# V's loads moved from SP's queue to ACT's in a cached attention decode kernel

## The chip, the cores and the metric

The kernel runs on one core of a Trainium2 chip. The metric is the device time of one execution in microseconds (us), median of several runs. Below, PE is TensorE (PEld its weight loads), DVE is VectorE, ACT is ScalarE, POOL is GpSimd and SP is SyncE. A transfer is issued by an engine, on that engine's own queue, and is carried out by the core's 16 DMA engines.

## The reference

For a batch of 2 with one new token each, the output is a gated mix of two branches:

```
g   = sigmoid(sum(x * gate_w))
a   = attention(x): q = x @ wq, 32 heads of 128
      p = softmax(q . k_cache / sqrt(128)) over 16384 cached positions
      a = (p @ v_cache) @ wo
b   = mlp(x): layernorm, w1, gelu, shifted w2, residual, layernorm, w3, gelu, w4, residual
out = g * a + (1 - g) * b
```

All inputs are bf16. `k_cache` and `v_cache` have the shape (2, 32, 16384, 128), 268 MB each: 573 MB are read with the weights, and each cached element is used once.

## The kernel before

**Units.** The work on the caches is cut into 32 units: 16 pairs of heads (`hp`) by 2 batch elements (`b`). A unit has one K transfer (`load_k`) and one V transfer (`load_v`) of 8.39 MB, each 128 rows of 64 KB, one to a partition. In the text a unit with b=0 is an even unit and one with b=1 an odd unit; K(hp,b) and V(hp,b) are their loads.

**Memory.** One SBUF tile `mem` is split into five cells of half a load. K of an even unit takes cells 0 and 1, K of an odd unit cells 1 and 2, so they share cell 1. V always takes cells 3 and 4. So K of the next unit can be loaded when the half of the present K that is in the way has been read, and V of the next unit when PV of the present one has read the cell.

**A unit's steps.** `score_first` and `score_second` go over K in halves: DVE turns a chunk (L408, eight to a unit), PE multiplies it with the spread-out query (L414) and sums into a PSUM tile S. `softmax_a` (L435 to L439) turns S, takes the maximum and writes the matrix `Dm` on ACT; `softmax_b` (L445 to L462) spreads the maximum over the partitions, makes the exps on ACT (L452) into `pt`, and takes the reciprocal of their sum on DVE (L462). `pv` (L468) is 64 matmuls of `pt` with V into `oacc`. `pv_end` evicts `oacc` on ACT (`osb`, L481) and sums it by matmuls (L486).

**Order.** The order of each engine is the program's (`in_order` ties each instruction to the one before it on its engine). The scores of one unit come ahead of PV of the unit before: after K of unit u has landed, the order is `score_first(u)`, the issue of K(u+1), `score_second(u)`, `softmax_a(u)`, `pv(u-1)`, the issue of V(u), `pv_end(u-1)`, `softmax_b(u)`. The loop `For_i` runs 15 times over `odd_rest` (from the second half of an odd unit) and `even_unit`; in its last round `last_unit` is added, and V(15,1) goes to cells 0 and 1.

**Queues.** All of K, V and the large weights are issued by SP, on its queue, in program order. An issue waits on SP until its place in `mem` is free (L112 for K, L117 for V). ACT issues only the two small inputs `xin` (L85) and `gwT` (L87) at the start. Before the loop, SP issues w1, w2, wq, K(0,0), w3, K(0,1) and V(0,0); after V(15,1) come wo and W4 in five pieces (`load_apart`, L526), which wait for PV of the units whose cells they take.

Of the kernel before, what the change touches and what calls it, by code (L numbers as in the profile page):

```python
# [23 lines left out]
def kernel(  # L24
# [15 lines left out]
    nc = tc.nc  # L40
    P = nc.NUM_PARTITIONS
    B, Sq, D = A_x.shape
    _, H, Sk, Dh = A_k_cache.shape
# [10 lines left out]
    NJ = 2 * Sk // P  # L54
# [25 lines left out]
    def region(cell, elements, offset=0):  # L80
        at = cell * CELL + offset
        return mem[:, at : at + elements]
# [24 lines left out]
    def cache_rows(cache, hp, b):  # L107
        two = cache[b, bass.ds(2 * hp, 2)]
        return two.rearrange("h s d -> (h s) d").rearrange("(p j) d -> p (j d)", p=P)
# [4 lines left out]
        )  # L114

    def load_v(hp, b, cell=V_CELL):
        nc.sync.dma_start(out=region(cell, NJ * Dh), in_=cache_rows(A_v_cache, hp, b))  # L117


    ident_f = const.tile([P, P], FP32)  # L120
# [3 lines left out]
        out=ident_s[:], in0=ident_f[:], scalar1=-scale, scalar2=None, op0=ALU.mult  # L124
# [10 lines left out]
        out=mask4[:], in_=mask4[:], compare_op=ALU.is_ge, fill=0.0,  # L135
# [3 lines left out]
        out=mask4[:], in_=mask4[:], compare_op=ALU.is_ge, fill=0.0,  # L139
# [11 lines left out]
        out=lmat[:].rearrange("p (g h k) -> p g h k", h=2, k=4),  # L151
        in_=hm2[:].unsqueeze(1).unsqueeze(3).to_broadcast([P, P // 8, 2, 4]),
# [5 lines left out]
        out=lane[:],  # L158
        in_=ident_f[:].rearrange("p (c k) -> p k c", k=QP),
# [5 lines left out]
    for g in range(Q4):  # L165
        nc.vector.tensor_scalar(
            out=spread[:, g],
# [161 lines left out]
    for k in range(2):  # L329
        wide = mlp.tile([P, 16, QP], FP32, tag="wide", name="wide")  # L330
        nc.scalar.activation(
            out=wide[:].rearrange("p (c e) i -> p c e i", e=2),
            in_=oacc[k][:].rearrange("p (c i e) -> p c e i", i=QP, e=2),
# [15 lines left out]
    for e in range(2):  # L349
        half = slice(e * HALF, (e + 1) * HALF)  # L350
        nc.vector.tensor_copy(
            out=qdu[half].rearrange("p u v -> p (u v)"),
            in_=qdps[half, e].rearrange("p k g n -> p (k g n)"),
# [212 lines left out]
    softmax_a(0)  # L566
    mlp_third(w3)
    load_v(0, 0)
    softmax_b(0)
    score_first(0, 1)  # L570
# [3 lines left out]
    def odd_rest(hp):  # L574
        loads.append(load_k(hp + 1, 0))
        score_second(1)
        softmax_a(1)
        pv(0)
        load_v(hp, 1)
        pv_end(hp, 0)  # L580
        softmax_b(1)

    def even_unit(hp):
        score_first(hp, 0)
        loads.append(load_k(hp, 1))
        score_second(0)
        softmax_a(0)
        pv(1)
        load_v(hp, 0)
        pv_end(hp - 1, 1)  # L590
        softmax_b(0)
        score_first(hp, 1)
# [89 lines left out]
```

## Time and profile before

| | |
|---|---|
| time, median of 3 runs | 1332.62 us (1332.56 to 1332.70) |
| the profiled execution's own time | 1332.68 us |
| its span, first to last instruction | 1330.5 us |
| busy: PE, DVE, ACT, POOL | 57%, 49%, 10%, 1% |
| read from HBM | 572.53 MB, 430 GB/s over the span |
| issue to landing, median: K, V | 28.0 us, 31.7 us |
| granted TensorE clock, mean | 0.794 |

The profile gives one execution. Its timeline lists instructions with their start, how long they took and, in brackets, how long the engine stood idle before and what ended that. `SPq` is SP issuing or waiting. A DMA's time to landing runs from its issue until its data is there, and includes the time behind other transfers. The trace also holds a record of every DMA packet with start, duration, size and queue; q1 is SP's queue and q10 is ACT's.

### The profile page before, as it was taken

The page shows a single profiled execution, that of the slowest core. Times are in us where ns is not written, and L with a number is a line of the kernel's source. Part 1 is how long each engine was busy: PE and PEld are TensorE (multiplying, and loading weights), DVE is VectorE, ACT ScalarE, POOL GpSimd, SP SyncE. Part 2 cuts the span into 40 slices and gives each one's busy share as a digit, 9 for nine tenths or more (in the row PEclk, how much of TensorE's full clock was granted, in tenths as well). Part 3 has the DMA queues.
Part 4 walks back from the last instruction along what each step waited for, and adds up shares of the span by engine and source line. Part 5 has one row for each costly group of instructions (what it writes and reads, how often), then busy time and mean ns, then how long its engine had stood idle before and what let it go on. Part 6 is the DMA issues. An engine that isn't in the chain of part 4 may idle for free.

```text
span 1330.5 us, 12949 instructions
## 1 busy us (share of the span) xinstructions
PE 763.4 (57%) x4992; PEld 330.0 (25%) x4992; DVE 654.0 (49%) x515; ACT 130.4 (10%) x204; POOL 13.0 (1%) x47
## 2 busy tenths in 40 slices
PE   1455666565556656555665655566565556656553
PEld 1222222222222222222222222222222222222222
DVE  2454455554445555444555544455554445555420
ACT  0011100011110001111000111110011111001110
POOL 1000000000000000000000000000000000000000
PEclk9777887687888868788886777888777788877776
DMA  9999999999999999999999999999999999999997
GB/s 410 432 434 426 436 437 433 428 435 437 435 426 435 437 435 426 435 437 435 426 435 437 435 426 435 437 435 428 433 437 437 426 433 437 437 426 433 437 437 333
DMA packets 11086, 572.69 MB, mean 430 GB/s; under 512 B 1602, under 2 KB 1602, under 8 KB 1988
## 3 DMA queue, kind: packets, MB, share of 16 engines
q1 hardware_dynamic: 10660, 572.53, 99.5%
q8 instruction: 8, 0.13, 0.0%
q10 hardware_dynamic: 416, 0.01, 0.0%
q14 instruction: 2, 0.02, 0.0%
HBM read 572.53 MB, written 0.00 MB: 430 GB/s over the span
## 4 chain that ended last, share of the span: by engine, by line
DMA 46%; PE 9%; DVE 8%; issue 5%; PEld 1%; DVEq 0%; ACT 0%; SPq 0%; PEldq 0%; ACTq 0%
DMA mem<-in_A_k_cache_dram 42%; PE S L414 8%; DVE KT L408 8%; DMA mem<-in_B_w_dram 2%; DMA mem<-in_A_v_cache_dram 2%; PE oacc L468 1%; PEld L414 0%; PEld misc L486 0%; ACT osb L481 0%; PEld misc L461 0%; SPq L112 0%; DVEq L408 0%; DVEq L641 0%; PEld misc L445 0%; DVEq L677 0%
## 5 line engine op out<-in xcount | busy, mean ns | idle before, releaser
L414 PE MATMUL S<-KT,qw 128*128 128x512 bf16 x2048 | 557.7, 424 | 354.9 <-DVE KT L408 348.4
L408 DVE STREAM_TRANSPOSE KT<-mem 128x2048 f32<-128x2048 f32 x256 | 574.2, 2287 | 270.6 <-DMA mem<-in_A_k_cache_dram 180.2
L414 PEld LDWEIGHTS <-qw 128*128 128x128 bf16 x2048 | 221.7, 108 | 686.0 <-issue 515.8
L468 PE MATMUL oacc<-mem,pt 128*8 128x512 bf16 x2048 | 118.9, 386 | 7.3 <-DMA mem<-in_A_v_cache_dram 7.3
L439 ACT ACTIVATE Dm<-ident_s,m 128x128 f32<-128x128 f32 x32 | 12.9, 402 | 979.1 <-PE oacc L468 915.0
L452 ACT ACTIVATE pt<-St,nb 64x256 bf16<-64x256 f32 x64 | 89.7, 1401 | 58.8 <-DVE nb L450 57.9
L490 DVE TENSOR_SCALAR o_all<-misc,g_rep 128x2 f32 (+1 forms) x32 | 7.0, 219 | 163.5 <-PE misc L486 163.5
L461 PE MATMUL misc<-rs,lmat 128*128 128x1 f32 x64 | 18.8, 362 | 106.8 <-ACT pt L452 61.2
L468 PEld LDWEIGHTS <-pt 128*8 128x8 bf16 x2048 | 47.5, 87 | 75.8 <-issue 24.3
L486 PE MATMUL misc<-lane,osb 128*128 128x2 f32 x256 | 33.3, 252 | 45.2 <-ACT osb L481 45.2
L462 DVE RECIPROCAL rinv<-misc 128x1 f32<-128x1 f32 x32 | 5.4, 168 | 107.4 <-PE misc L461 104.2
L435 DVE STREAM_TRANSPOSE St<-S 128x512 f32<-128x512 f32 x32 | 22.9, 716 | 66.2 <-PE L468 64.2
L486 PEld LDWEIGHTS misc<-lane,osb 128*128 128x128 f32 x256 | 31.0, 191 | 60.9 <-ACT osb L481 31.6
L461 PEld LDWEIGHTS misc<-rs,lmat 128*128 128x128 f32 x64 | 16.0, 311 | 113.1 <-ACT pt L452 64.8
L481 ACT ACTIVATE osb<-oacc,rinv 128x512 f32<-128x512 f32 x32 | 22.0, 687 | 88.6 <-PE oacc L468 88.6
L452 ACT ACTIVATION_READ_ACCUMULATOR pt<-St,nb 64x1 f32 x64 | 30.5, 477 | 0.0
L357 POOL TENSOR_TENSOR qw<-qdu,mask 128x16 bf16<-128x16 bf16 x32 | 8.5, 267 | 1162.4 <-PE L468 1089.8
L450 DVE TENSOR_REDUCE nb<-misc 64x1 f32<-64x64 f32 x64 | 14.2, 222 | 4.8 <-PE misc L445 0.7
L445 PE MATMUL misc<-Dm,ones_f 128*128 128x128 f32 x64 | 15.4, 323 | 0.0
L370 PE MATMUL arow<-mem,o_turned 128*2 128x256 bf16 x128 | 5.9, 361 | 14.7 <-DMA mem<-in_A_wo_dram 8.9
L437 DVE TENSOR_REDUCE m<-St 128x1 f32<-128x256 f32 x32 | 13.4, 420 | 1.1
L551 DVE CAST out_row<-arow 2x256 bf16<-2x256 f32 x2 | 0.8, 414 | 26.1 <-PE arow L370 26.1
(85 smaller groups left out, 73.6 us busy)
## 6 DMA issues: line engine op xcount, KB each, us to landing
mem<-in_B_w_dram SPq DMA_DIRECT2D x1, 7168.0 KB, 32.6
mem<-in_B_w_dram SPq DMA_DIRECT2D x2, 2048.0 KB, 12.2
mem<-in_B_w_dram SPq DMA_DIRECT2D x1, 3840.0 KB, 41.3
mem<-in_B_w_dram SPq DMA_DIRECT2D x1, 1792.0 KB, 30.8
mem<-in_B_w_dram SPq DMA_DIRECT2D x1, 768.0 KB, 32.2
mem<-in_A_k_cache_dram SPq DMA_DIRECT2D x32, 28.0
mem<-in_A_v_cache_dram SPq DMA_DIRECT2D x32, 31.7
mem<-in_B_w_dram SPq DMA_DIRECT2D x1, 512.0 KB, 33.0
```

The costliest lines, as they stand in the source:

```text
L408: nc.vector.transpose(out=kt[:], in_=Kc.rearrange("p j d -> p (j d)").bitcast(FP32))
L414: nc.tensor.matmul(S, lhsT=qw[b][:, v, NG - 1 - m : NG - 1 - m + P], rhs=ktb[:, half * GT : (half + 1) * GT, w, :, e], start=(first and n ...
L435: nc.vector.transpose(out=st[:].rearrange("p j r -> p (j r)"), in_=S[:])
L437: nc.vector.tensor_reduce(out=m[:], in_=st[:, :, 0:NG], axis=AX.XY, op=ALU.max)
L439: nc.scalar.activation(out=Dm[:], in_=ident_s[:], func=ACTF.Copy, scale=m[:, 0:1])
L445: nc.tensor.matmul(R_ps[:], lhsT=ones_f[:], rhs=Dm[:], start=True, stop=True)
L450: nc.vector.tensor_reduce(out=nb[rows], in_=R_ps[rows, rows], axis=AX.X, op=ALU.min)
L452: nc.scalar.activation(out=pts[b][rows, :, e, :].rearrange("p (m a) k -> p a k m", a=GT // 4), in_=st[rows, :, 0:NG].rearrange("p (a k) m ...
L461: nc.tensor.matmul(tot_ps[:], lhsT=lmat[:], rhs=rs[:], start=True, stop=True)
L468: nc.tensor.matmul(oacc[b][QP * q : QP * q + 8, :], lhsT=pts[b][:, g].rearrange("p h k -> p (h k)"), rhs=V[:, 4 * g : 4 * g + 4, :].rearra ...
L481: nc.scalar.activation(out=osb[:], in_=oacc[b][:], func=ACTF.Copy, scale=rinvs[b][:, 0:1])
L486: nc.tensor.matmul(ot[:], lhsT=osb[:, k * Dh : (k + 1) * Dh], rhs=lane[:, k : k + 5 : 4], start=(k == 0), stop=(k == 3),)
```

## The change

`load_v` issues its transfer from ACT in the place of SP. Source, destination, size and the place in the program's order stay; the waits on V's cell stand on ACT now, in ACT's order. All 32 V transfers are meant, V(15,1) in `last_unit` too. K's and the weights' transfers stay with SP.

```
     def load_v(hp, b, cell=V_CELL):
-        nc.sync.dma_start(out=region(cell, NJ * Dh), in_=cache_rows(A_v_cache, hp, b))
+        nc.scalar.dma_start(out=region(cell, NJ * Dh), in_=cache_rows(A_v_cache, hp, b))
```

## The prediction

> **What bounds the kernel now.** I read the page first: DMA share by slice, the queues, the chain.
>
> ```profile
> DMA  9999999999999999999999999999999999999997
> ...
> q1 hardware_dynamic: 10660, 572.53, 99.5%
> ...
> DMA mem<-in_A_k_cache_dram 42%; PE S L414 8%; DVE KT L408 8%; DMA mem<-in_B_w_dram 2%; DMA mem<-in_A_v_cache_dram 2%; PE oacc L468 1%; PEld L414 0%; PEld misc L486 0%; ACT osb L481 0%; PEld misc L461 0%; SPq L112 0%; DVEq L408 0%; DVEq L641 0%; PEld misc L445 0%; DVEq L677 0%
> ```
>
> SP's queue (q1) fills the 16 DMA engines for 99.5% of the span, and every slice but the last reads nine tenths. No compute engine passes 57%. The kernel is DMA-bound; its time changes only if the DMA engines stand empty for longer or shorter, or move bytes at another rate. What is empty now is 0.5% of 1330.5, 6.7 us, and it lies at the two ends: nothing moves before 1.8 us or after the last weight piece (below).
>
> Next, what the queue waited for (SP's waits), and one odd unit (b=1) and the even one after it in the timeline:
>
> ```profile
> SPq L112 <- DVE KT L408: 489.0, 31, 23.4
> SPq L117 <- PE oacc L468: 345.7, 30, 17.8
> ```
>
> ```profile
> 477.08 4.51 DVE L408 STREAM_TRANSPOSE KT<-mem 128x2048 f32<-128x2048 f32 x2 [6.87 <-DMA mem<-in_A_k_cache_dram]
> ...
> 487.76 0.34 SPq L112 DMA_DIRECT2D mem<-in_A_k_cache_dram  x1
> ...
> 501.83 3.63 PE L468 MATMUL oacc<-mem,pt 128*8 128x512 bf16 x64
> ...
> 506.12 0.33 SPq L117 DMA_DIRECT2D mem<-in_A_v_cache_dram  x1
> ...
> 512.15 0.17 DVE L462 RECIPROCAL rinv<-misc 128x1 f32<-128x1 f32 x1 [3.35 <-PE misc L461]
> 515.78 4.51 DVE L408 STREAM_TRANSPOSE KT<-mem 128x2048 f32<-128x2048 f32 x2 [3.46 <-DMA mem<-in_A_k_cache_dram]
> ...
> 525.88 0.33 SPq L112 DMA_DIRECT2D mem<-in_A_k_cache_dram  x1
> ```
>
> Read from K's landing (477.08): the next K is issued 10.7 us later, when half of this K is transposed (10.1 to 11.5 over the units); PV runs 24.8 later, V is issued 29.0 later, DVE is free 35.2 later. Landings are 38.70 us apart, two loads of 19.35: the queue always holds the next load while one moves. Each load is 128 rows of 64 KB, so 8 packets per DMA engine at 2.42 us.
>
> Last, what two queues do to each other, in the DMA queues' view and in stretches of time (last two columns: DMA share, GB/s; a packet counts whole where it starts):
>
> ```profile
> xin<-in_A_x_dram ACTq DMA_DIRECT2D x1, 4.0 KB, 12.9
> gwT<-in_gate_w_dram ACTq DMA_DIRECT2D x1, 2.0 KB, 31.8
> ```
>
> ```profile
> 0.80:1.80 1.00, 0.00 (x0) 0.00 (x0) 0.38 (x4) 0.00 (x0) 0.79 (x5) 1.00 0.00 0
> 1.80:2.20 0.40, 0.00 (x0) 0.00 (x0) 0.28 (x4) 0.00 (x0) 0.40 (x2) 1.00 3.02 573
> ...
> 13.00:32.40 19.40, 6.10 (x72) 3.85 (x72) 4.66 (x25) 0.98 (x3) 1.41 (x2) 1.00 1.00 433
> ```
>
> 2 KB on ACT's queue took 31.8 us: its 9 small packets per engine each waited for one large packet of SP's. So the engines take turns, one packet from each queue. While that went on (13.0 to 32.4) SP's rate was the usual 433 GB/s: turning costs nothing that shows. SP's first issue is at 0.80 and the first packet follows in the 1.80 stretch: 1.0 us from issue to motion.
>
> **The change, part by part.**
>
> *Issue cost.* 32 transfers leave SP and join ACT. Each is 0.33 us of DMA_DIRECT2D with a register move (0.03) and a register operation (0.07): 0.43 us on ACT, 13.8 us in all, on an engine busy for 10%. ACT's wait before V (PV's end) is the one its next instruction, the eviction osb at L481, has anyway (506.11 against V's 506.12); behind it stand osb, the exps and so the reciprocal. That path ends 35.2 after K's landing, 3.5 before the next K, so 0.43 would hide there. In the new order (below) it holds up K's transposes in even units, and V's seventh packet covers it; uncovered, 16 × 0.43 = 7. On SP, K's issue loses the V wait ahead of it, worth nothing: K's last wait was for DVE (row one).
>
> *Order of the bytes.* This carries the sum. Before, K and V moved one after the other; now whichever overlap share packet by packet, so a K takes up to twice as long, and either queue can run dry alone. The engines stand empty only when both are dry: V's queue is dry from V's last byte until PV is over, K's from K's last byte until half of K is transposed. Worked through in packets:
>
> At the start: w3 ends at 70.1, K(0,1) then moves, V(0,0) (issued at 77.9, moving at 78.8) joins when K has 4 packets left. Eight alternating packets, 19.4 us, bring K in at 99.6 instead of 89.96, and V has 4 left, 9.7 us, until 108.8. K(1,0) can't move before 99.6 + 10.9 + 0.9 = 111.4. Empty: 2.6.
>
> In the loop, with 0 the last byte of an odd unit's K (0.47 before DVE starts, by the packet records), and V having 5 packets left, to 12.1:
> - Next K moves at 0.47 + 10.8 + 0.9 = 12.2 (0.9 lies between 1.04 for the first weight and 0.74 for the output in the packet records), alone: V is issued at 29.5 and moves at 30.4, in K's last packet. K lands at 31.6.
> - V moves alone with 8 packets. The even unit can't start: DVE is free at 35.2 + 0.47 = 35.7, 36.1 with ACT's 0.43. Its next K moves at 36.1 + 10.6 + 0.9 = 47.6, waits for V's seventh packet (48.5), alternates with the eighth; V lands at 53.4.
> - PV waits for the scores and V is issued 25.4 after the unit's start (24.9 to 26.1 in even units), at 61.5, and moves at 62.4, within K's fifth packet (to 63.1). Three K and three V packets alternate: K lands at 77.6, V has 5 left. The pattern repeats; 77.6 against 77.4 before.
>
> So an odd unit's V is drained at 12.1 and K comes at 12.2 in the middle, 11.5 to 13.0 at the ends of the rows: empty 0 to 0.9, mean near 0.2. After a standstill the first packets are slow: 0.95 to 1.76 us at the start of the run against 0.61 for the same size later, so 0.3 to 1.1 more; I take 0.35 on average, since often K comes without a full stop. 14 odd units after the first: 14 × 0.55 = 7.7. The start costs 2.6 + 0.5 = 3.1. Sum +10.8.
>
> The price of issue to motion decides. The Trainium skill ("DMA: Bandwidth & Descriptors", section "Latency and other measured facts") puts a first byte from SP or ACT at about 0.6 us; the rows here show 0.74 and 1.04. By 0.6, K would come at 11.9, before V has drained, and only the start's 2.8 would remain, 1335.5; I go by the rows.
>
> *Tail.* V(15,1) now shares with wo instead of going before it. PV of it ends before wo and the first W4 piece are through (28 us), so the later pieces still come in time: zero; if that cover fails, PV's 6.5 us plus 1 of issue.
>
> **Rivals.**
> 1. *No change* (within 0.2%, 2.7 us, about what a measurement of this kernel can tell from no change). K reaches the engines before 12.1, or K's turn comes slightly more often than V's, and the loop never runs dry: 0 to 2.6 for the start, about 1334.5. For it: K came at 11.5 in some units. Against: the middle is over 12.1, and one standstill delays K and feeds the next. The Trainium skill's rule in the same page ("Issuing engines are not separate DMA queues") also gives no change: all issuers' transfers run on the same 16 engines and interleave, only issue time is saved. The xin row bears out the interleaving; the rule says nothing of when a queue runs dry.
> 2. *Much slower.* One V packet fewer is left at the odd landing (4, drained at 9.7): K is 2.5 late plus 0.5 of refill, in 14 units, 42, with the start 45: 1378. It decides if V's next load moves a packet earlier, before 60.6 instead of 62.4, or if engines share finer than by packets: in even shares without whole packets the same steps give 1.5 to 2.0 per pair, 21 to 28 and the start, near 1360.
> 3. *Faster.* Two queues fill gaps between packets of one. Against: 8 × 2.419 is 19.35, there are no gaps between loads; the 6.7 us empty now lie where one transfer or none is under way. If the first 1.8 and half the 4.7 after the last byte came back, -4: 1328.5, but V's queue touches neither end.
> 4. *The transfers stay in one order whatever the queue*: the time stays, 1332.7. The gwT row speaks against it; its chance is in "no change".
>
> **How the numbers follow.** Forecast 0.55, rival 2 0.20, no change 0.17, faster 0.08. The profiled execution took 1332.68 (span 1330.5, 2.2 around it), the median is 1332.62, so no correction: 1332.7 + 10.8 = 1343.5. Its own bounds: issue to motion of 0.74 with no refill gives +3.5; 1.3 with 0.5 gives +17. The range, 1333.5 to 1365, takes in the upper part of "no change" and the finer sharing. Faster 0.08, same 0.17, slower 0.75.
>
> **What would show it.** V on ACT's queue (q10) with 268 MB; landings of K in turn about 32 and 46 us apart instead of 38.7; K's time to landing near 20 and 31, V's 24 and 28; slices around 430 GB/s; a first K landing in the loop near 99.6. Wrong if landings still come every 38.7 (one order), if DMA slices hold 433 all along (no change), or if they drop under 425 (rival 2).

## The result and the profile after

The time goes from 1332.66 us to 1357.21 us (medians of 4 runs each; the change ranges from 1355.97 to 1357.46): ratio 1.0182, interval 1.0170 to 1.0195. It is slower, by 24.6 us where 10.8 were forecast. The profiled execution took 1357.46, span 1355.3, 24.8 more than the one before.

The page of the changed kernel: DMA share and rate by slice, the two queues, the chain.

```profile
DMA  9999989999999999999999999999999999999998
GB/s 403 431 437 403 434 371 433 433 429 433 406 433 402 433 433 429 435 404 433 426 435 408 433 433 433 433 402 433 433 433 433 402 433 433 433 404 435 435 427 342
...
q1 hardware_dynamic: 6052, 304.09, 52.7%
q10 hardware_dynamic: 5024, 268.44, 45.9%
...
DMA mem<-in_A_k_cache_dram 49%; DVE KT L408 9%; PE S L414 7%; DMA mem<-in_B_w_dram 2%; DMA mem<-in_A_v_cache_dram 2%; PE oacc L468 0%; PEld L414 0%; DVEq L408 0%; DVEq L641 0%; PEld misc L486 0%; SPq L112 0%; PEld misc L461 0%; DVEq L677 0%; DVE out_row L551 0%; PE arow L370 0%
```

V's 268 MB are on ACT's queue (q10). Most slices still move 433 GB/s, but nine between the first and the last drop to 371 to 408. The DMA queues' view shows that K now takes longer to land (28.0 before) and V less (31.7 before):

```profile
mem<-in_A_k_cache_dram SPq DMA_DIRECT2D x32, 32.3
mem<-in_A_v_cache_dram ACTq DMA_DIRECT2D x32, 29.2
```

The timeline around an odd unit, the even one after it and the next odd one:

```profile
652.75 4.50 DVE L408 STREAM_TRANSPOSE KT<-mem 128x2048 f32<-128x2048 f32 x2 [11.54 <-DMA mem<-in_A_k_cache_dram]
...
663.55 0.34 SPq L112 DMA_DIRECT2D mem<-in_A_k_cache_dram  x1
...
676.46 3.63 PE L468 MATMUL oacc<-mem,pt 128*8 128x512 bf16 x64
...
680.76 0.34 ACTq L117 DMA_DIRECT2D mem<-in_A_v_cache_dram  x1
681.28 0.69 ACT L481 ACTIVATE osb<-oacc,rinv 128x512 f32<-128x512 f32 x1 [2.92 <-PE oacc L468]
...
687.28 0.17 DVE L462 RECIPROCAL rinv<-misc 128x1 f32<-128x1 f32 x1 [3.35 <-PE misc L461]
688.00 4.50 DVE L408 STREAM_TRANSPOSE KT<-mem 128x2048 f32<-128x2048 f32 x2 [0.55 <-DMA mem<-in_A_k_cache_dram]
...
731.54 4.50 DVE L408 STREAM_TRANSPOSE KT<-mem 128x2048 f32<-128x2048 f32 x2 [11.57 <-DMA mem<-in_A_k_cache_dram]
```

DVE starts on K at 652.75, 688.00 and 731.54: 35.3 and 43.5 apart where both were 38.7. The pair takes 78.8 instead of 77.4. osb starts 0.52 after V's issue on ACT. What happens just after 663.55 is seen in stretches of the same execution (last two columns: DMA share, GB/s; a packet counts whole in the stretch it starts in):

```profile
655.00:663.90 8.90, 8.28 (x27) 3.07 (x27) 6.87 (x4) 0.00 (x0) 0.00 (x0) 0.74 0.82 353
663.90:664.50 0.60, 0.60 (x5) 0.24 (x4) 0.00 (x0) 0.00 (x0) 0.00 (x0) 1.00 0.01 0
664.50:665.10 0.60, 0.60 (x4) 0.17 (x2) 0.00 (x0) 0.00 (x0) 0.00 (x0) 1.00 3.90 1311
```

By the packet records, the last V packets end one engine after the other from 663.8 to 664.4, and no packet of a load starts in the second row's 0.6 us. From 664.5 to 665.6 the 16 engines take up the K that SP issued at 663.55. This comes back once in every pair, and the first K packets are slow then: 12 to 16 of the 16 take over 0.3 us more, and the mean over the pairs is 3.06 us instead of 2.42 (0.64 more). In the same execution, the first packets of a K that joins a running V (703.7, even unit) are not slow: 2.42 us.

The records show one thing more. A load is complete when each engine has also served a 4-byte packet behind its data, and that packet takes its own turn in the queue. With one queue K landed 0.1 us after its last data; here, wherever V is moving, the small packet waits behind one 64 KB packet of V (2.41 us), and K lands 2.7 to 2.8 us after its last data. The sum over the middle of the run, in stretches from 110 to 1280 us, before and then after:

```profile
110.00:1280.00 1170.00, 695.88 (x4282) 298.49 (x4281) 599.41 (x426) 118.91 (x184) 7.76 (x29) 0.80 1.00 433
```

```profile
110.00:1280.00 1170.00, 672.10 (x4168) 290.74 (x4168) 584.59 (x416) 116.90 (x180) 7.70 (x29) 0.80 0.99 425
```

8 of 433 GB/s over 1170 us are 21.6 us. The share falls by only 0.01, because an engine with a slow first packet counts as busy.

### The profile page after: what moved, and what is told of

It reads as the page before. It is cut to its first block, busy times and chain, and to the rows that moved or that the text cites. A ratio compares the mean times of both kernels' runs of the same rounds, so it can differ in the third digit from the quotient of the medians.

```text
span 1355.3 us, 13000 instructions
## 1 busy us (share of the span) xinstructions
PE 755.5 (56%) x4992; PEld 329.2 (24%) x4992; DVE 651.7 (48%) x515; ACT 130.4 (10%) x204; POOL 12.9 (1%) x47
## 4 chain that ended last, share of the span: by engine, by line
DMA 53%; DVE 9%; PE 8%; issue 4%; PEld 0%; DVEq 0%; SPq 0%; PEldq 0%; ACTq 0%
DMA mem<-in_A_k_cache_dram 49%; DVE KT L408 9%; PE S L414 7%; DMA mem<-in_B_w_dram 2%; DMA mem<-in_A_v_cache_dram 2%; PE oacc L468 0%; PEld L414 0%; DVEq L408 0%; DVEq L641 0%; PEld misc L486 0%; SPq L112 0%; PEld misc L461 0%; DVEq L677 0%; DVE out_row L551 0%; PE arow L370 0%
## 5 line engine op out<-in xcount | busy, mean ns | idle before, releaser
L414 PE MATMUL S<-KT,qw 128*128 128x512 bf16 x2048 | 548.0, 417 | 375.7 <-DVE KT L408 370.4
L439 ACT ACTIVATE Dm<-ident_s,m 128x128 f32<-128x128 f32 x32 | 12.9, 402 | 990.4 <-PE oacc L468 908.6
L206 DVE STREAM_TRANSPOSE turn<-wide 128x256 f32<-128x256 f32 (+2 forms) x5 | 3.4, 685 | 18.1 <-ACT wide L331 10.7
(85 smaller groups left out, 78.4 us busy)
## 6 DMA issues: line engine op xcount, KB each, us to landing
mem<-in_B_w_dram SPq DMA_DIRECT2D x2, 2048.0 KB, 12.2
mem<-in_A_k_cache_dram SPq DMA_DIRECT2D x32, 32.3
```

The source lines that it names most:

```text
L414: nc.tensor.matmul(S, lhsT=qw[b][:, v, NG - 1 - m : NG - 1 - m + P], rhs=ktb[:, half * GT : (half + 1) * GT, w, :, e], start=(first and n ...
L439: nc.scalar.activation(out=Dm[:], in_=ident_s[:], func=ACTF.Copy, scale=m[:, 0:1])
```

## The experiments

**Theory A**: the queues take packets in turn; in an odd unit both run dry before the next K moves, the engines stand and restart slowly. **Rivals**: B, V's issue on ACT and what stands behind it makes the loss; C, two transfers under way at once move fewer bytes per us. D to H name rivals of single runs. The rate below is that of 110 to 1280 us.

### K and V exchanged: e1_swap and e12_swap_loop

```
     def load_k(hp, b):
-        return nc.sync.dma_start(
+        return nc.scalar.dma_start(            # V: nc.sync, as before
```

> K's transfers on ACT's queue, V's back on SP's: still two queues, but no V issue on ACT. Theory A (the two queues take packets in turn, and both run dry in an odd unit before the next K moves): the loss stays, 1350 to 1361 us, with standstills and K landings about 35 and 43.5 us apart. Rival B (ACT's 0.4 us of issue ahead of the eviction, 32 times, and what stands behind it, makes the loss): about 1333 to 1340, as K's issue stands where ACT has nothing to do. Rival C (two transfers under way at once move fewer bytes per us): as A in time, but with a rate under 433 GB/s in the stretches without a standstill.

Measured: 1377.9 us (1372.5 to 1381.6), ratio 1.0335. Outside A's range too: K(0,1) now waits in ACT's order, and the engines are empty from 32.1 to 40.3 and from 77.1 to 90.3. After that most pairs are 78.4 to 78.9 us long. So it was run again with K(0,0) and K(0,1) on SP (`load_k` now takes the issuing engine as an argument):

```
-    load_k(0, 0)
+    load_k(0, 0, nc.sync)                      # and load_k(0, 1, nc.sync)
```

> As e1_swap (K on ACT's queue, V on SP's), but the two K loads ahead of the loop stay on SP, since in e1_swap they waited in ACT's order and left the engines empty for 7.9 and 13 us before 91 us. A: the loop's pairs stay 78.5 us long and the whole is 1352 to 1360 us. B (the loss is ACT's issue of V ahead of the eviction): 1333 to 1340.

Measured: 1357.5 us (1356.3 to 1361.8), ratio 1.0183 (1.0168 to 1.0199), the changed kernel's own. V isn't issued by ACT here at all, so B falls: the loss belongs to two queues, not to V's issue on ACT. The row is of the slowest of the four executions, 1361.8 us.

```profile
110.00:1280.00 1170.00, 665.66 (x4144) 287.02 (x4144) 577.97 (x413) 116.90 (x180) 7.72 (x29) 0.80 0.99 423
```

### The next K later: e4_late_k, and on one queue e5_late_k_one_queue

```
-        score_chunks(b, halves[1 - b], True, False)
+        score_chunks(b, [0, 1, 2, 4] if b else halves[1], True, False)
...
     def odd_rest(hp):
+        score_chunks(1, [3], False, False)
         loads.append(load_k(hp + 1, 0))
-        score_second(1)
+        score_chunks(1, [5, 6, 7], False, True)     # the same in last_unit
```

> The changed kernel with one other chunk of K scored ahead of the last chunk of the shared cell in odd units, so that the next K is issued one chunk and the loop's turn later, 4.6 us. A: the standstill of 0.4 grows to about 5 us per pair where whole packets don't hide some: 30 to 60 us on top, 1385 to 1415 us. B and C: nothing about ACT or about shared movement changes, 1357 to 1360.

> The control to e4_late_k: the same later issue of K (4.6 us in odd units) with all on SP's queue. A: V is under way when K is issued, so the 4.6 us are hidden: 1332.5 to 1333.5 us. If a later K costs by itself (E), 15 x 4.6: about 1400 us.

Measured: e4 1391.0 us (1389.9 to 1394.0), ratio 1.0443, 33.8 more than the changed kernel; e5 1338.4 (1334.3 to 1339.6), ratio 1.0043. The slices of e4 show the larger standstills, in rates down to 336 GB/s and shares of seven and eight tenths:

```profile
DMA  9998979999999999989999999989999999999997
GB/s 416 428 427 373 440 336 442 404 423 423 393 423 404 442 393 423 440 376 451 395 423 393 423 423 393 438 378 451 395 423 425 404 440 387 429 393 423 453 421 336
```

In the loop they are mostly 2 to 3 us by the packet records, against 0.3 to 0.8. The wait for the next K is therefore the price in two queues, as A has it. The control missed slightly: one queue hides most of the 4.6 us, but 1.7 to 7 us remain. A likely reason, argued and not shown: K then moves about 17 us after the last byte, and the engine that is 2.1 us ahead of the last one has drained its V at 17.3.

### V in smaller packets: e2_half_v, e3_quarter_v, e11_half_v_one_queue

```
     def load_v(hp, b, cell=V_CELL):
-        nc.scalar.dma_start(out=region(cell, NJ * Dh), in_=cache_rows(A_v_cache, hp, b))
+        rows = cache_rows(A_v_cache, hp, b)
+        n = NJ * Dh // 2                            # // 4 in e3; nc.sync in e11
+        for k in range(2):
+            nc.scalar.dma_start(out=region(cell, n, k * n), in_=rows[:, k * n : (k + 1) * n])
```

> The changed kernel with each V load cut into two halves along the row, 32 KB packets in the place of 64 KB: in turns of one packet K moves 64 KB for V's 32, so V lasts longer beside K. A: V still has packets when the next K comes in every unit, the standstills go, 1332 to 1336 us. B: 32 more issues on ACT, 1357 or up to 14 more. C: as many bytes or more move beside each other, 1357 or more.

> The changed kernel with each V load in four quarters, 16 KB packets: V gets a fifth of the engines while K moves, so V ends late, PV and the next V wait for it, and K runs alone and dry. A: slower than the changed kernel, 1365 to 1430 us, estimated by steps in packets. B: 96 more issues on ACT at 0.4 us, 1357 to 1395, with no late V. C: about 1357 (the bytes that move beside each other change little).

> The kernel before, all on SP's queue, with V in two halves along the row (32 KB packets): what the smaller packets cost by themselves. In e2_half_v a 32 KB packet took 1.213 us against half of 2.4194, 1.2097: over 8192 packets on 16 engines 1.7 us, up to the 3.1 that its records sum to. So 1334.4 to 1336 us if the rest of e2_half_v's 13 us comes from its two queues (A); 1343 to 1346 if halves cost that much on any queue (D).

Measured: e2 1346.1 us (1343.4 to 1348.3), ratio 1.0105; e3 1349.5 (1346.4 to 1356.0), ratio 1.0142; e11 1334.6 (1334.5 to 1334.8), ratio 1.0015 (1.0006 to 1.0024). So halves cost 2.0 by themselves, and two queues with halves lose 11.5 more, less than half of the changed kernel's loss. That is right in direction, short in size: long standstills are gone (none over 0.3 us in e2's loop, as a mean over the 16 engines), but many engines still drain V just as K comes, and 142 K packets are over 0.3 us slow (223 in the changed kernel). Halves do two things, and these runs don't separate them: V lasts longer beside K, and K's completion waits behind 32 KB of V (1.21 us) in the place of 64 KB (2.41). In e3 my estimate was wrong: V doesn't end late, since it has the engines to itself while the next K waits. In its profiled execution (13.7 us over before) 9.7 are the 16 KB packets' own: 0.614 us each against 0.605, a quarter of 2.4194. B and C don't fit either: more issues on ACT, or as much sharing, made it faster.

### Half a K ahead of time: e6_split_k, e14_split_k_one_queue, e16_split_even_k, e17_split_odd_k

```
     def load_k(hp, b):
-        return nc.sync.dma_start(
-            out=region(K_CELL[b], NJ * Dh), in_=cache_rows(A_k_cache, hp, b)
-        )
+        rows = cache_rows(A_k_cache, hp, b)
+        parts = []
+        for k in (b, 1 - b):                        # the half for the cell that only this K uses, first
+            parts.append(nc.sync.dma_start(
+                out=region(K_CELL[b], CELL, k * CELL), in_=rows[:, k * CELL : (k + 1) * CELL]))
+        return parts
```

e6 has V in halves on ACT too; e14 has V whole on SP. e16 splits only K of b=0 (e17: of b=1), with V whole on ACT:

```
+        cells = ((b,), (1 - b,)) if b == 0 else ((0, 1),)      # one DMA for each group of cells; e17: b == 1
```

> The changed kernel with K loaded in halves by cell: the half for the cell that no other K uses is issued as soon as that cell is read, before the present K has landed; the other half as before. V in halves too, so that packets stay of one size. SP's queue then always holds half a K when V has drained. A: no standstills, no slow restarts in the loop: 1333 plus 2 x 3 for the 32 KB packets plus up to 3 at start and tail, 1336 to 1343 us. C (two transfers under way at once are slower): 1357 or more.

> The control to e6_split_k: K in halves by cell, all on SP's queue, V whole. Only the smaller packets cost, as V's halves did (2.0): 1334 to 1335.5 us. Then e6_split_k's 5.2 us are 4.0 of packets and about 1 that two queues cost where neither runs dry.

Measured: e6 1337.8 us (1336.8 to 1338.1), ratio 1.0038 (1.0025 to 1.0051); e14 1334.7 (1334.6 to 1334.9), ratio 1.0015 (1.0006 to 1.0024). K and V are still on two queues and under way together, yet the rate is back:

```profile
110.00:1280.00 1170.00, 716.14 (x4210) 303.37 (x4209) 594.80 (x422) 116.87 (x180) 7.73 (x29) 0.80 1.00 432
```

By the packet records no stretch of e6's loop is empty. C falls. Of its 5.2 us, 2.0 and 1.9 are the halves (e11, e14); 1.3 are left for two queues that don't run dry.

> The changed kernel with only the K loads of even units in halves by cell (those that are issued in odd units), the half for the free cell issued early; V whole. A (the loss comes from the next K moving too late in the odd units, after V has drained): the standstills and slow restarts go, 1.0 us for the smaller packets: 1333 to 1341 us. If the loss is spread over all units (G): about half of it is left, 1343 to 1350.

> The mirror of e16_split_even_k: only the K loads of odd units in halves, those that are issued in even units. A: the odd units' next K still comes after V has drained: 1352 to 1362 us. G: about half of the loss is left, 1343 to 1350.

Measured: e16 1352.2 us (1351.1 to 1352.9), ratio 1.0148; e17 1363.4 (1359.4 to 1364.0), ratio 1.0223. G falls with both. e17 lies 1.4 us above A's range, in A's direction: standstills at V's end stay in odd units, in about every second pair, most of them 1.2 to 4.4 us long. e16 missed: the standstills of odd units at V's end go, but now V's first packets are slow (149 of them over 0.3 us), and where V came late the engines stood empty (3.8 us at 442). With half a K ahead, K ends sooner, in the odd unit by 680.6, just when V, issued after PV, comes at 678.6 to 680.6. So "the odd units' K alone" was too narrow. Both queues wait for compute in each unit, and when one wait is taken away the other becomes the place where both are dry.

### A shorter wait: e15_three_kt, and both measures: e18_kt_half_v

```
-    ktpool = ctx.enter_context(tc.tile_pool(name="ktpool", bufs=2))
+    ktpool = ctx.enter_context(tc.tile_pool(name="ktpool", bufs=3))
...
-        osb = ppool.tile([P, 4 * Dh], FP32, name="osb")
+        osb = mlp.tile([P, 4 * Dh], FP32, tag="wide", name="osb")
```

e18 adds the two halves of V from e2.

> The changed kernel with three KT buffers in the place of two (the eviction osb takes the place of a buffer that is no longer used, to make room): DVE's first four transposes of a K run without waiting for PE, so half of K is read 4 x 2.28 + 0.2 = 9.3 us after landing instead of 10.6, and the next K is issued 1.2 us earlier. A: K moves before V has drained, the standstills of 0.4 and most of the slow restarts go: 1334 to 1346 us. B and C: no change, 1356 to 1358.

> The changed kernel with three KT buffers (K issued 1.6 us earlier) and V in halves (V lasts longer beside K). A, if each part measure only moved the edge: together they take K clear of V's end: 1335 to 1343 us, 2.0 of it for the packets. If the place where it settles follows the measures (H), as either alone: 1343 to 1353.

Measured: e15 1353.1 us (1347.5 to 1355.7), ratio 1.0145; e18 1335.9 (1335.0 to 1338.0), ratio 1.0026 (1.0016 to 1.0036). K was issued 9.1 us after landing in e15 (10.7 in the changed kernel):

```profile
649.13 4.50 DVE L408 STREAM_TRANSPOSE KT<-mem 128x2048 f32<-128x2048 f32 x2 [10.75 <-DMA mem<-in_A_k_cache_dram]
```

```profile
658.22 36.14 SPq L112 DMA_DIRECT2D mem<-in_A_k_cache_dram  x2
```

That returned 4, not the 11 or more expected; 188 K packets stay slow. Together with V's halves (e2 returned 11.1 alone) nearly all comes back: 3.3 us over before, 2.0 of them packets, with 3 K packets over 0.3 us slow in the whole run, and no empty stretch before the tail.

```profile
110.00:1280.00 1170.00, 699.10 (x4248) 306.35 (x4250) 593.41 (x423) 117.05 (x181) 7.77 (x29) 0.78 1.00 432
```

H falls; either measure alone leaves the kernel near the edge, both take it clear. The edge can be read in the packet records: in the loop's odd units K is issued 0.3 to 1.4 us before V's last byte in the changed kernel, 2.5 or more in e15 and 4.5 or more in e18, and only the last has next to no slow first packets. No version was faster than the kernel before, whose DMA engines are idle only at its ends.

### The ends undone: e9_last_v_sp, e10_first_v_sp

```
-        load_v(hp, 1, V_LAST)
+        load_v(hp, 1, V_LAST, nc.sync)              # e9; in e10: load_v(0, 0, V_CELL, nc.sync)
```

> The changed kernel with V(15,1) alone back on SP's queue, ahead of wo as before. A: the loop keeps its loss; at the tail V(15,1) no longer shares with wo, and of the 1.9 us more that the engines stand empty at the end (6.2 against 4.3) up to all come back: 1355 to 1357.5 us. If the tail hides more of the loss than that (F), under 1354.

> The changed kernel with V(0,0) alone on SP's queue, behind K(0,1) as before. A: the first standstill (1.3 us at 107, with a slow restart of 0.7) goes, and the second (3.9 at 187, 0.7) falls to the loop's usual 0.4 or is shifted a pair: 1351 to 1357 us.

Measured: e9 1357.5 us (1355.3 to 1358.6), e10 1357.6 (1357.3 to 1360.0), ratios 1.0184 and 1.0192. Neither returns anything that these runs can tell, and e10's lies above its range. In e10 the two large standstills (1.3 at 107 and 3.9 at 187 us in the changed kernel) are there again, 3.8 at 146 and 1.7 at 267. They belong to the approach to the steady pattern, wherever it begins, not to V(0,0).

## Why the prediction was right in kind and too small

*What bounds the kernel, the issue cost, the turns.* Right. ACT's issue holds up osb by 0.52 us (0.43 forecast), and it costs nothing that shows (e12). Packets alternate one for one, and the pattern of the walk is there: landings 32.3 to 32.8 and 46.0 to 47.3 us apart from 132 to 416 us (32 and 46 forecast), and about 35 and 43.5 later, where V comes early enough to put a packet ahead of K's completion. V has 5 packets left at an odd landing, as forecast, but that is partly luck. The walk left out that the completion waits for a packet of V, and also that a load that joins a running one lets one more of its packets pass than the walk had: in the pair shown, V joins with 2 K packets to go, not 3. Each moves the count by one packet, in opposite directions.

*The forecast's own case held, its terms were mis-sized.* The packet records of the two profiled executions give, in us (empty is a mean over the 16 engines; another way of counting the overlaps moves the sum by about 1):

| term of the sum | forecast | measured |
|---|---|---|
| start, with restarts | 3.1 | 6.6 (1.3 and 3.9 empty, 0.7 and 0.7 of slow packets) |
| empty in the 14 pairs | 14 × 0.2 = 2.8 | 7.5 (mostly 0.3 to 0.8; one of 1.6) |
| slow packets in the 14 pairs | 14 × 0.35 = 4.9 | 9.4 (0.67 a pair, V's few included) |
| tail | 0 | 1.9 (6.2 empty against 4.3) |
| sum | 10.8 | 25.4, against 24.8 between the spans |

Two terms came out at twice their size or more. The larger miss is the empty time: 5.4 forecast (2.6 at the start, 2.8 in the pairs), 12.7 measured, and 1.9 more in the tail. In the pairs it comes from taking V's end and K's start as two single moments. Counted from the prediction's 0 (0.47 us before DVE starts), V ends between 11.5 on the first engine and 12.2 on the last, 11.8 on average (12.1 forecast), and K starts between 12.2 and 12.9, 12.4 on average (12.2 forecast); these are means over 13 pairs. So issue to motion is 0.96 to 0.99 us for the first engine, 1.4 to 2.0 for the last and 1.2 on average, where the prediction had 0.9 from where the first packet starts. The Trainium skill's 0.6 us for a first byte ("DMA: Bandwidth & Descriptors", section "Latency and other measured facts") would have made the sum smaller still; it agrees with these records only if it is counted from the end of the issuing instruction, which takes 0.34 us here.

The second is the restart: 5.4 forecast (0.5 and 4.9), 10.8 measured. I took 0.35 "since often K comes without a full stop". In every pair 12 to 16 of the 16 engines have a slow first packet, even where the engines stand empty for only 0.3 us on average. The price was within the bounds I had (0.3 to 1.1), and I chose low.

In the start I walked through one standstill and went straight to the steady pattern. The approach has a second and larger one, and e10 shows that it can't be taken away at that end. The tail was costed at nothing; 1.9 us of emptiness are there, but they don't come from where V(15,1) is issued: e9 has it back on SP, and 5.9 us of its tail are empty.

*The rivals.* "No change" fails in its mechanism: K doesn't come before V drains in the loop. The Trainium skill's rule that all issuers' transfers run on the same 16 engines and interleave ("DMA: Bandwidth & Descriptors", section "Issuing engines are not separate DMA queues") is borne out where neither queue runs dry: e6 and e18 are within 0.4% of before. It doesn't cover what was lost here, 24.6 us. "Much slower" gave 45 for one packet fewer, which didn't happen in the loop; its second price, sharing finer than by packets, came to 1360, near the result but by another mechanism: the packets do stay whole. "Faster" and "one order" didn't happen.

*What stays open.* Why V's lead over K settles at that edge is argued from the walk only: in a pair without loss V's lead at the odd landing falls by the 2 to 3 us by which V is issued later in odd units (27.9 to 29.0 us after K's landing, against 25.3 to 25.9 in most even ones), until the standstill makes up for it. That e15 returned so little agrees with it; no run shows it by itself. What makes a first packet slow is open too: the slow ones start soon after their issue on engines that mostly had nothing to do, and no run separates the two.

## What to carry to other kernels

When one queue already keeps the DMA engines full, a second one added no bytes in any run here, but it can take away the cover that order gave: a late issue was hidden behind the other stream's transfer, and now it is hidden only by what that stream has left. Count for each stream the time from its landing to the motion of its next load (compute until the place is free, issue to the last engine's first packet, and a slow first packet), and to its landing add the turn that its completion waits behind the other stream's packet. Then check that the other stream still has that much in its queue at that moment. If two queues are wanted, split the loads so that a part can be issued before the place of the rest is free, or change the packet sizes to shift the shares; and relieve both streams, since relieving one moves the standstill to the other.

## What the runs showed of the hardware

- Two queues of 64 KB packets were served one packet each in turn, with 2.42 us a packet as on one queue.
- The completion of a load takes a turn of its own: beside 64 KB packets of the other queue it came 2.41 us after the last data, beside 32 KB packets 1.21 (e2, e18).
- From an issue on SP to the first packet 0.96 to 0.99 us on the first engine and 1.4 to 2.0 on the sixteenth when V was ending (odd units); 3.4 to 5.5 us to the first packet when V was still running (even units).
- After a standstill, the first 64 KB packets took 0.64 us more on average; the profile counts that as busy (share 0.99 at 425 GB/s, against 1.00 at 433).
- Smaller packets are slightly dearer: 2.419 us for 64 KB, 1.213 to 1.218 for 32 KB, 0.614 for 16 KB. V's 268 MB in 32 KB packets took 2.0 us more (e11).
